# A three-stage kernel (attention, eight experts, gated MLP) with its attention reordered, its index scatters spread, and its MLP weight decoding regrouped

## The chip, the cores and the metric

The kernel runs on one core of one Trainium2 chip. Its time is the device time of one execution in microseconds (us); three runs of the kernel before took 479.15, 480.61 and 486.78 us, median 480.61. The engines are PE (TensorE, matrix products), DVE (VectorE), ACT (ScalarE), POOL (GpSimd) and SP (SyncE, which here only issues transfers). Each takes its instructions in program order.

## The reference

```python
def reference(**kw):
    # 1. linear attention with decay w and bonus u; batch 2, heads 8, 768 tokens, head size 48
    #    y[t] = r[t] @ (state + u*k[t] v[t]^T);  state = w*state + k[t] v[t]^T
    x = attn(r, k, v, w, u)                       # -> 1536 tokens x 384
    # 2. mixture of experts, top 1 of 8, a capacity per expert, hidden 1024
    e, g = argmax(x @ moe_w_gate), softmax value of that expert
    out[i] = g[i] * relu(x[i] @ w1[e[i]]) @ w2[e[i]]      # 0 for tokens over capacity
    # 3. gated MLP, 384 -> 1536 -> 384
    return (sigmoid(out @ w_gate) * (out @ w_val)) @ w_out
```

The three weights of stage 3 come as 64-bit numbers (`wy`, two 32-bit words each), and the kernel decodes them to 32-bit floats on the chip.

## The kernel before

**Attention** works in eight steps `s` (two batches `b` of four head pairs). For each step three tiles are loaded: `dm` (r and k by channel), `kr` (k and r by token) and `v`. `rp` and `kb` scale `dm` by the decay, `pr_part`, `sums` and `diag` build the diagonal term, `kk_part` the keys of the state. On PE `a_mm` makes scores (tile `ap`), `a_cp` copies them on DVE under a mask into `at`, `u_pe`/`u_t` make the running state (`tbd`), `t_mm` and `v_mm` the output, `out_evac`, `out_tr` and `out_x` bring it out and transposed, with router logits `lg` beside it. `r1`, `r2`, `r3` turn the logits of a batch into expert, rank and gate weight; `r4` scales a 128-token block (`xs`) and scatters its rows into the buffer `xs_d` in DRAM, with an indirect DMA issued from POOL. `zinit` first writes zeros there, eight times, in the steps that `ZI` gives. `pre` loads the rows of expert 0 from batch 0 (`xr0`), and `first` adds the ones of batch 1 with 0/1 matrices `pick`, so that expert 0 need not wait for the second batch's scatters. Products with `zero` (`warm_up`, `FILL`) are dummy work for PE.

**Experts**: 64 steps `i` (eight experts of eight slices). Each does `s1` (9 products of 256 columns) and, four steps later, `s2` (9 more). Values are split in a high part (ACT copy) and a low part (subtraction), three products for each. Weight tiles arrive as `raw`; `bg` splits one per step into `rh` (ACT) and `rl` (DVE, in odd steps after 8 POOL); eight are converted ahead. `eload` loads the rows of a later expert (`xr`), `etr` transposes them. `c1`, `c2` compute where each token stands in the sorted order; twelve scatters write the token numbers to `ids_d` (128 numbers of 4 bytes each), one per step from step 4. Beside this the first seven MLP weights (`EARLY`) are decoded, one operation of `decode` per step.

**MLP**: 48 gates, `mf` (18 products of 384 columns), `gate` (`sg` on ACT, `gg` on DVE, `gh` on ACT, `gl` on DVE) and `mo` (9 products). One PSUM pair `pg` serves nearly all gates, so the next `mf` waits for `gg`. Two lanes of gates run skewed by `SKEW` = 2, so the first two rounds hold one gate each. One of the eleven remaining weights is decoded per round: `o1` (ACT), `o2` to `o5` (DVE), `o6` (ACT copy, POOL subtraction), `o7` fetches another weight.

The order is the program's own (`tc.manual_schedule()`).

Of the kernel before, what the change touches and what calls it, by code (L numbers as in the profile page):

```python
# [34 lines left out]
BG = (0, 0, 0, 0, 0, 0, 4, 3)  # L35
DP = 2
ORDER = (0, 1, 2, 12, 3, 4, 13, 5, 6, 14, 7, 8, 15, 9, 10, 16, 11, 17)
EARLY = 7
# [3 lines left out]
R4A = [3, 5]  # L42
R4S = [3]
EB0 = (5, 6)
EB = (1, 4)
# [57 lines left out]
def body(tc, A, out):  # L103
    nc = tc.nc
    E = mybir.EngineType
    with ExitStack() as top, tc.manual_schedule():
# [44 lines left out]
        def decode(n):  # L151
            t = {}

            def o1():
                t["a"] = spl[0].tile([128, 768], F32, tag="wf", name="wf", bufs=2)
                t["i"] = t["a"].bitcast(I32)
                nc.scalar.activation(out=t["a"], in_=r64[n][:, :, 1].bitcast(F32), func=AF.Abs, scale=2.0 ** 16)  # L157
# [27 lines left out]
            return [o1, o2, o3, o4, o5, o6, o7]  # L185
# [20 lines left out]
        tri = gp_.tile([128, 128], BF16, tag="tri", name="tri")  # L206
# [14 lines left out]
        with ExitStack() as ctx:  # L221
# [9 lines left out]
            iw = cat[:, 776:1320].rearrange("p (a x) -> p a x", x=136)  # L231
            wd = cp.tile([112, 4], F32, tag="wd", name="wd")
# [141 lines left out]
            def t_mm(s, fill=0):  # L374
                if s == 7:
                    for g in range(2):
                        y7[g] = ps.tile([128, 512], F32, tag="a", name="y7")
                else:
                    Y0[s] = pb.tile([128, 512], F32, tag="big", name="y0")
# [4 lines left out]
                for c in range(1, 6):  # L384
                    nc.tensor.matmul(y_out(s, c), tbd[s % 2][:, c - 1, :], D[s][:, 0, c * 128:(c + 1) * 128],
                                     start=c in (1, 4) or (s == 7 and c == 2), stop=False, skip_group_check=True)

            def v_mm(s, cs=range(6)):
                for c in cs:
                    o = y_out(s, c)  # L390
                    for h in range(2):
                        nc.tensor.matmul(o[64 * h:64 * h + 64], V[s][:, c, h, :], AT[s][:, slot(c, h), :], start=False,
                                         stop=(h == 1), skip_group_check=True)

# [58 lines left out]
            def r2(b):  # L453
                x, m2, oh, se = R[b]
                rk = ps.tile([128, 6, 8], F32, tag="a", name="rk")
# [10 lines left out]
            def r3(b):  # L466
# [9 lines left out]
                pi = rt.tile([128, 6], I32, tag="pi", name="pi")  # L476
                nc.gpsimd.tensor_scalar_add(pi, pf, 12288.0)
                R[b] = [x, m2, oh, rank, pi, gk]
                pfs[b] = pf

# [4 lines left out]
            def first():  # L485
                x, m2, oh, rank, pi, gk = R[1]
                xk = [pb.tile([128, 512], F32, tag="big", name="xk")[:, 0:256] for _ in range(3)]
# [7 lines left out]
                for c in range(6):  # L495
                    (nc.gpsimd if c > DP else nc.vector).tensor_scalar(
                        out=pick[:, c * 256:c * 256 + 256], in0=cat[:, 512:768], scalar1=pfs[1][:, c:c + 1],
                        scalar2=None, op0=ALU.is_equal)
                hl = []
                for c in range(6):  # L500
# [7 lines left out]
                    if c in R4A:  # L508
                        r4(1, R4A.index(c), "s")
                    nc.vector.scalar_tensor_tensor(out=lo, in0=x[:, c, :], scalar=gk[:, c:c + 1], in1=hi.bitcast(F32),  # L510
                                                   op0=ALU.mult, op1=ALU.subtract)
                order = [(c, kt, p) for b in (0, 2) for p in range(2) for c in (b, b + 1) for kt in range(3)]
# [54 lines left out]
            nc.sync.dma_start(out=cat[:, 512:1320], in_=A["cax"])  # L567
            nc.scalar.dma_start(out=capi, in_=A["cap"][:, 0:1].partition_broadcast(128))
            P_.memset(zero, 0.0)
            for i in range(2):  # L570
                P_.memset(kkd[i][:, :, :, 48:64], 0.0)
# [14 lines left out]
            pr_part(0, (P_, V_))  # L586
# [4 lines left out]
            kb(1, P_)  # L591
            rp(1)
            warm_up(W1)
            u_pe(0)
            u_t(0)
            warm_up(W2)
            pr_part(1, (P_, V_))
            sums(1)
            a_cp(0, ap)
            kk_part(1)  # L600
            diag(1)
            load(2, "v")
            load(3, "k")
            rest = []

            for s in range(8):
# [10 lines left out]
                if s == 0:  # L617
                    kb(2, P_)
                    rp(2)
                    t_mm(0, FILL[0])  # L620
                    ap = a_mm(1)
                    v_mm(0)
                    u_pe(1)
                    pr_part(2, (P_, V_))
                    sums(2)
                    kk_part(2)
                    a_cp(1, ap)
                    diag(2)
                    u_t(1)
                    pr_part(3, (P_, P_))  # L630
                    continue
                out_evac(s - 1)
# [3 lines left out]
                if s > 5:  # L636
                    bg(BG[s], False, 0, rest)
                if s == 7:
                    for o, a, b in rest:
                        nc.vector.tensor_sub(o, a, b)  # L640
# [3 lines left out]
                if nx:  # L644
                    ap = a_mm(s + 1)
                if fu:
                    kb(s + 2, P_)
                    kk_part(s + 2)
                    if s < 5:
                        pr_part(s + 3, (P_, P_))  # L650
                    diag(s + 2)
                if nx:
                    a_cp(s + 1, ap)
                t_mm(s, FILL[s])
# [10 lines left out]
                if s == 5:  # L665
                    r2(0)
                    r3(0)
                    for c in RS[5]:
                        r4(0, c, "v")
                if s == 6:  # L670
                    for o, a, b in rest:
                        nc.vector.tensor_sub(o, a, b)
# [337 lines left out]
```

## Time and profile before

| stretch | us | PE busy | granted clock |
|---|---|---|---|
| attention, to the first product of the experts | 98.07 | 79.59 | 0.91 |
| experts | 143.55 | 138.74 | 0.99 |
| MLP, to the last gate's products | 221.43 | 217.70 | 1.00 |
| last outputs | 15.85 | 10.43 | 0.95 |

The profiled execution took 480.61 us; its span is 478.9 us. PE is busy 446.5 us (93%), DVE 280.6 (59%), ACT 220.8 (46%), POOL 184.5 (39%). A granted clock of 1.00 is TensorE's 2.4 GHz, 0.50 its 1.2 GHz. A line of the timeline gives the start, the duration, the engine, the line of the kernel, and in brackets how long the engine sat idle before it and what ended that.

### The profile page before, as it was taken

The page shows a single profiled execution, that of the slowest core. Times are in us where ns is not written, and L with a number is a line of the kernel's source. Part 1 is how long each engine was busy: PE and PEld are TensorE (multiplying, and loading weights), DVE is VectorE, ACT ScalarE, POOL GpSimd, SP SyncE. Part 2 cuts the span into 40 slices and gives each one's busy share as a digit, 9 for nine tenths or more (in the row PEclk, how much of TensorE's full clock was granted, in tenths as well). Part 3 has the DMA queues.
Part 4 walks back from the last instruction along what each step waited for, and adds up shares of the span by engine and source line. Part 5 has one row for each costly group of instructions (what it writes and reads, how often), then busy time and mean ns, then how long its engine had stood idle before and what let it go on. Part 6 is the DMA issues. An engine that isn't in the chain of part 4 may idle for free.

```text
span 478.9 us, 8621 instructions
## 1 busy us (share of the span) xinstructions
PE 446.5 (93%) x3354; PEld 431.4 (90%) x3356; DVE 280.6 (59%) x474; ACT 220.8 (46%) x450; POOL 184.5 (39%) x127
## 2 busy tenths in 40 slices
PE   6978988599979999999989899999999999999995
PEld 2777987599979999999979799999999999999995
DVE  4797997668778788889347676566222221212221
ACT  2676877536736777675332433433232322222231
POOL 4876938735885647467111311221120200000022
PEclk9979999799989999999999999999999999999999
DMA  7999951779898787773012312310010100000011
GB/s 213 347 340 309 273 203 72 248 288 216 197 227 305 269 271 238 254 258 101 3 47 86 133 66 75 124 68 0 1 49 1 49 1 0 1 1 0 1 50 49
DMA packets 23707, 65.10 MB, mean 136 GB/s; under 512 B 4592, under 2 KB 8816, under 8 KB 23664
## 3 DMA queue, kind: packets, MB, share of 16 engines
q1 hardware_dynamic: 21600, 59.80, 40.5%
q0 software_dynamic: 1920, 4.73, 2.7%
q8 instruction: 27, 0.44, 0.4%
q14 instruction: 16, 0.13, 0.1%
q10 hardware_dynamic: 144, 0.00, 0.0%
HBM read 56.65 MB, written 7.87 MB: 135 GB/s over the span
## 4 chain that ended last, share of the span: by engine, by line
PE 44%; DVE 3%; issue 3%; ACT 1%; POOL 1%; POOLq 0%; DVEq 0%; ACTq 0%
PE pg L936 28%; PE po L960 5%; PE po L959 5%; PE po L958 5%; DVE wf L160 1%; PE ph L825 1%; PE py L848 1%; DVE gg L943 1%; POOL out_dram L190 1%; PE py L849 1%; PE py L850 1%; DVE wf L167 1%; ACT wf L157 1%; DVE wf L171 0%; DVE gl L947 0%
## 5 line engine op out<-in xcount | busy, mean ns | idle before, releaser
L943 DVE TENSOR_TENSOR gg<-sg,pg 128x384 f32<-128x384 f32 x48 | 26.5, 553 | 93.6 <-PE pg L936 91.6
L139 POOL TENSOR_TENSOR rl<-raw,rh 128x768 fp32r<-128x768 f32 x26 | 52.1, 2006 | 36.0 <-ACT rh L137 35.9
L936 PE MATMUL pg<-xhi,ws 128*128 128x384 f32 x240 | 61.6, 337 | 4.6 <-ACT sg L941 3.0
L946 ACT CAST gh<-gg 128x384 fp32r<-128x384 f32 x48 | 24.7, 514 | 83.9 <-DVE gg L943 83.9
L190 POOL DMA_INDIRECT out_dram<-ob,ids x12 | 11.7, 976 | 123.8 <-ACT ob L967 121.4
L941 ACT ACTIVATE sg<-pg 128x384 f32<-128x384 f32 x48 | 23.5, 490 | 70.6 <-PE pg L936 70.6
L848 PE MATMUL py<-hh,rh 128*128 128x256 f32 x192 | 54.6, 284 | 0.0
L137 ACT CAST rh<-raw 128x768 fp32r<-128x768 f32 x64 | 51.4, 836 | 4.7 <-PE py L849 1.9
L849 PE MATMUL py<-hl,rh 128*128 128x256 f32 x192 | 53.5, 279 | 0.0
L850 PE MATMUL py<-hh,rl 128*128 128x256 f32 x192 | 53.5, 278 | 0.0
L139 DVE TENSOR_TENSOR rl<-raw,rh 128x768 fp32r<-128x768 f32 x31 | 46.3, 1497 | 10.6 <-ACT rh L137 10.5
L936 PE MATMUL pg<-xlo,rh 128*128 128x384 f32 x144 | 48.7, 338 | 0.0
L936 PE MATMUL pg<-xhi,rh 128*128 128x384 f32 x144 | 48.6, 338 | 0.0
L936 PEld LDWEIGHTS pg<-xhi,ws 128*128 128x128 f32 x240 | 43.0, 188 | 6.1 <-ACT sg L941 3.7
L936 PE MATMUL pg<-xhi,rl 128*128 128x384 f32 x144 | 48.5, 337 | 0.0
L947 DVE TENSOR_TENSOR gl<-gg,gh 128x384 fp32r<-128x384 f32 x48 | 26.8, 558 | 27.8 <-ACT gh L946 27.8
L936 PE MATMUL pg<-xlo,ws 128*128 128x384 f32 x120 | 40.2, 335 | 0.0
L178 POOL TENSOR_TENSOR rl<-wf,rh 128x768 fp32r<-128x768 f32 x8 | 14.7, 1840 | 65.4 <-ACT rh L177 59.9
L848 PEld LDWEIGHTS py<-hh,rh 128*128 128x128 f32 x192 | 36.4, 189 | 0.1
L850 PEld LDWEIGHTS py<-hh,rl 128*128 128x128 f32 x192 | 36.5, 190 | 0.0
L849 PEld LDWEIGHTS py<-hl,rh 128*128 128x128 f32 x192 | 36.5, 190 | 0.0
L327 ACT ACTIVATE at<-cst,dl 128x128 f32<-128x128 f32 x96 | 28.9, 387 | 7.6 <-DVE dl L319 7.5
(187 smaller groups left out, 1211.9 us busy)
## 6 DMA issues: line engine op xcount, KB each, us to landing
raw<-in_wx_dram SPq DMA_DIRECT2D x64, 384.0 KB, 5.6
r<-in_wy_dram SPq DMA_DIRECT2D x18, 768.0 KB, 4.5
dm<-in_dm_dram SPq DMA_DIRECT2D x8, 672.0 KB, 11.6
kr<-in_kr_dram SPq DMA_DIRECT2D x8, 576.0 KB, 11.6
v<-in_v_dram SPq DMA_DIRECT2D x8, 384.0 KB, 10.9
xs_d<-zero SPq DMA_DIRECT2D x8, 384.0 KB, 10.5
xr<-xs_d SPq DMA_DIRECT2D x8, 384.0 KB, 4.1
cat<-in_cax_dram SPq DMA_DIRECT2D x1, 404.0 KB, 13.8
```

The costliest lines, as they stand in the source:

```text
L137: nc.scalar.copy(out=h, in_=t)
L139: (nc.gpsimd if pool else nc.vector).tensor_sub(rl[n % NR], t, h.bitcast(F32))
L327: nc.scalar.mul(AT[s][:, j, :], ident, dl[:, j:j + 1])
L848: nc.tensor.matmul(y, wh[:, w], hh, start=(f == 0 and m != 1), stop=False, skip_group_check=True)
L849: nc.tensor.matmul(y, wh[:, w], hl, start=False, stop=False, skip_group_check=True)
L850: nc.tensor.matmul(y, wl[:, w], hh, start=False, stop=(f == 7), skip_group_check=True)
L936: nc.tensor.matmul(pg[g], a[:, w], b[kt][:, c], start=(kt == n == 0), stop=(kt == last and n == 2))
L943: nc.vector.tensor_mul(gg, sg, pg[1])
L946: nc.scalar.copy(out=gh, in_=gg)
L947: nc.vector.tensor_sub(gl, gg, gh.bitcast(F32))
L958: nc.tensor.matmul(po[j][t], gh[:, a], wh[:, w], start=(f == 0), stop=False)
L959: nc.tensor.matmul(po[j][t], gh[:, a], wl[:, w], start=False, stop=False)
```

## The change

Settings: the zeros are written in later steps (`ZI`), weights are converted later (`BG`: 2 and 3 instead of 4 and 3), decoding starts at expert step 8 (`T0`), expert 1's rows are transposed at steps 6 and 7 (`EB0`), those of expert 2 two steps later (`EB`). In attention, operations of the first steps move between POOL and DVE and change places, the last step's products change places (`last_open`, `last_t`), batch 0's ranks are made a step earlier in the program's step 5, dummy products (`idle`) come before and after the last ranks, and all `pick` go to DVE. Expert 1's rows are loaded from POOL's queue. The index scatters go to every fourth step from 12. `wf`, the tile of a weight being decoded, gets a third buffer, its low part is made on DVE (`o8`), and the MLP decodes two weights in three gates.

```diff
-T0 = 6
-RS = {5: (0, 1, 2), 6: (3, 4, 5)}
+T0 = 8
+RS = {5: (0, 1), 6: (2, 3, 4, 5)}
+IDLE = (10, 4)
-W2 = 12
-FILL = (0, 4, 4, 4, 4, 4, 4, 8)
-ZI = (4, 4, 0, 0, 0, 0, 0, 0)
+W2 = 20
+FILL = (4, 4, 4, 4, 4, 4, 4, 8)
+ZI = (0, 1, 2, 3, 2, 0, 0, 0)
-BG = (0, 0, 0, 0, 0, 0, 4, 3)
+BG = (0, 0, 0, 0, 0, 0, 2, 3)
-EB0 = (5, 6)
-EB = (1, 4)
+EB0 = (6, 7)
+EB = {1: (3, 6)}
...
-                t["a"] = spl[0].tile([128, 768], F32, tag="wf", name="wf", bufs=2)
+                t["a"] = spl[0].tile([128, 768], F32, tag="wf", name="wf", bufs=3)
...
-                nc.gpsimd.tensor_sub(wyl[n], t["a"], wyh[n].bitcast(F32))
+            def o8():
+                nc.vector.tensor_sub(wyl[n], t["a"], wyh[n].bitcast(F32))
...
             if s == 0:
                     kb(2, P_)
+                    pr_part(2, (P_, P_))
+                    ap = a_mm(1)
+                    t_mm(0, FILL[0])
+                    a_cp(1, ap)
                     rp(2)
-                    t_mm(0, FILL[0])
-                    ap = a_mm(1)
+                    kk_part(2)
                     v_mm(0)
                     u_pe(1)
-                    pr_part(2, (P_, V_))
                     sums(2)
-                    kk_part(2)
-                    a_cp(1, ap)
-                    diag(2)
+                    out_evac(0)
                     u_t(1)
+                    diag(2, 3)
...
                 if nx:
                     ap = a_mm(s + 1)
+                if s == 5:
+                    r2(0, ap[3][:, 256:304].rearrange("p (a b) -> p a b", a=6))
+                    r3(0)
...
             pre()
+            last_open()
+            v_mm(7)
+            for o, a, b in rest:
+                nc.vector.tensor_sub(o, a, b)
+            for g in range(3):
+                last_t(g)
+                last_evac(g)
+            out_tr(6)
+            out_tr(7)
+            xk = [pb.tile([128, 512], F32, tag="big", name="xk") for _ in range(3)]
+            idle(IDLE[0])
+            out_x(6)
             out_x(7)
             r1(1)
...
+                cnt(1)
+                bg(BG[7])
...
-            dops = [op for n in ORDER[:EARLY] for op in decode(n)]
+                dops += [d[0], d[1], d[2], d[3], d[4], d[6], lambda d=d: (d[5](), d[7]())]
-            eload(1)
-            dfetch(ORDER[0])
-            dfetch(ORDER[1])
+            eload(1, nc.gpsimd)
...
-                    if i >= 4 and nid < 12:
+                    if i >= 12 and i % 4 == 0 and nid < 12:
                         scatter(sci, "sci", ids_d, cpos[:, nid:nid + 1], tid[:, nid:nid + 1], 1536)
...
+            def groups():
+                work = [decode(n) for n in ORDER[EARLY:]]
+                a, b = None, None
+                for i in range(0, len(work) + 2, 2):
+                    n, m = (work[j] if j < len(work) else [lambda: None] * 8 for j in (i, i + 1))
+                    yield [n[0]] + ([b[5], a[7]] if a else []) + [n[1], n[2]] + ([b[7]] if a else [])
+                    yield [m[0], n[3], n[4], n[6], m[1]]
+                    yield [n[5], m[2], m[3], m[4], m[6]]
+                    a, b = n, m
...
             for k in range(24 + SKEW):
-                ops = decode(todo.pop(0)) if todo else []
-                for op in ops[:3]:
-                    op()
                 if k < 24:
                     gate(*lane(0, k), mf(*lane(0, k)))
                 if 0 < k <= 24:
                     mo(*lane(0, k - 1))
-                for op in ops[3:5]:
-                    op()
+                if k < 24:
+                    some()
                 b = k - SKEW
                 if b >= 0:
                     gate(*lane(1, b), mf(*lane(1, b)))
+                    some()
```

ACT at the entry of the MLP, before (`xhi` is the last expert's output, `wf` the operation `o1`, `rh` the copy `o6`):

```order
L854 COPY xhi_1303<-py 128x256
L157 ACTIVATE wf<-r_2762 128x768
L941 ACTIVATE sg<-pg 128x384
L946 CAST gh<-gg 128x384
L177 CAST rh_68<-wf 128x768
L157 ACTIVATE wf<-r_2966 128x768
```

The same place on ACT in the change:

```order
L889 COPY xhi_1319<-py 128x256
L979 ACTIVATE sg<-pg 128x384
L984 CAST gh<-gg 128x384
L157 ACTIVATE wf<-r_2799 128x768
L979 ACTIVATE sg<-pg 128x384
L984 CAST gh<-gg 128x384
L157 ACTIVATE wf<-r_3003 128x768
L979 ACTIVATE sg<-pg 128x384
L984 CAST gh<-gg 128x384
L177 CAST rh_68<-wf 128x768
```

The copy of the first weight moved from behind the first gate to behind the third, and no `wf` stands ahead of the first.

DVE at the end of attention, before (`rl` are low parts of expert weights, `lg` the last logits):

```order
L672 TENSOR_TENSOR rl_76<-raw,rh_68 128x768
L672 TENSOR_TENSOR rl_77<-raw,rh_69 128x768
L672 TENSOR_TENSOR rl_78<-raw,rh_70 128x768
L672 TENSOR_TENSOR rl_79<-raw,rh_71 128x768
L640 TENSOR_TENSOR rl_80<-raw,rh_72 128x768
L640 TENSOR_TENSOR rl_81<-raw,rh_73 128x768
L640 TENSOR_TENSOR rl_82<-raw,rh_74 128x768
L425 TENSOR_TENSOR lg<-lg,xp 128x24 x2
```

In the change, the same place and then the start of the experts:

```order
L698 TENSOR_TENSOR rl_76<-raw,rh_68 128x768
L698 TENSOR_TENSOR rl_77<-raw,rh_69 128x768
L412 COPY yt<-y_1092 128x256
L438 TENSOR_TENSOR lg<-lg,xp 128x24 x4
...
L538 TENSOR_TENSOR xel<-xk,xeh 128x256 x3
L552 TENSOR_REDUCE cnts<-oh 128x8
L139 TENSOR_TENSOR rl_78<-raw,rh_70 128x768
L139 TENSOR_TENSOR rl_79<-raw,rh_71 128x768
L139 TENSOR_TENSOR rl_80<-raw,rh_72 128x768
L869 SCALAR_TENSOR_TENSOR hl<-ph,hh 128x512
```

Two subtractions stand ahead of the last logits where seven stood; three moved behind expert 0's rows (`xel`), ahead of the first `hl`.

POOL from the second batch's scatters on, before:

```order
L496 TENSOR_SCALAR pick<-cat,pf 128x256 x3
L190 DMA xs_d<-xs,pi 12288x384 x6
L190 DMA ids_d<-tid,cpos 1536x1 x3
L883 TENSOR_LOAD mxi
L190 DMA ids_d<-tid,cpos 1536x1 x3
L139 TENSOR_TENSOR rl_81<-raw,rh_73 128x768
```

POOL in the change:

```order
L192 DMA xs_d<-xs,pi 12288x384 x6
L830 DMA xr<-xs_d 128x2x384
L921 TENSOR_LOAD mxi
L139 TENSOR_TENSOR rl_81<-raw,rh_73 128x768
L139 TENSOR_TENSOR rl_83<-raw,rh_75 128x768
L192 DMA ids_d<-tid,cpos 1536x1
```

The picks are gone from POOL, the load of expert 1's rows stands in its queue, and the index scatters come one at a time between subtractions.

## Rows read from the trace of the kernel before

**Rows 1.** Stretches: busy time of each engine, clock, DMA share, GB/s.

```profile
0.00:98.07 98.07, 79.59 (x863) 67.33 (x865) 74.14 (x183) 63.88 (x177) 69.83 (x59) 0.91 0.80 254
98.07:241.62 143.55, 138.74 (x1198) 137.57 (x1196) 111.50 (x151) 87.78 (x145) 82.68 (x46) 0.99 0.72 213
241.62:463.05 221.43, 217.70 (x1238) 216.42 (x1239) 92.41 (x136) 65.89 (x123) 27.69 (x19) 1.00 0.11 39
```

**Rows 2.** PE's waits in attention: total us, times, longest.

```profile
PE xk L490 <- DMA xr<-xs_d: 4.4, 1, 4.4
...
PE ap L336 <- DMA v<-in_v_dram: 2.1, 1, 2.1
```

**Rows 3.** PE in order of time, attention: start, duration, line, idle before.

```profile
27.49 3.39 PE L359 MATMUL ap<-dm 48*128 48x128 f32 x24 [2.72 <-DVE at L366]
...
37.26 1.61 PE L359 MATMUL ap<-dm 48*128 48x128 f32 x24
...
46.07 1.61 PE L359 MATMUL ap<-dm 48*128 48x128 f32 x24
...
59.56 1.61 PE L359 MATMUL ap<-dm 48*128 48x128 f32 x24
...
68.12 1.61 PE L359 MATMUL ap<-dm 48*128 48x128 f32 x24
...
74.22 0.61 PE L392 MATMUL t<-at,v 128*64 128x128 f32 x8
...
77.70 1.56 PE L411 MATMUL xp<-cat,yt 128*128 128x136 f32 x12
79.18 1.09 PE L392 MATMUL y<-at,v 128*64 128x128 f32 x16
...
98.07 1.01 PE L825 MATMUL ph<-xeh,rh 128*128 128x256 f32 x3
```

**Rows 4.** Clock in two stretches of 2 us; columns as in Rows 1.

```profile
92.00:94.00 2.00, 2.00 (x11) 2.00 (x11) 0.20 (x1) 0.00 (x0) 1.39 (x3) 0.50 0.95 343
136.00:138.00 2.00, 2.00 (x12) 2.00 (x11) 1.27 (x2) 0.52 (x2) 1.93 (x2) 0.52 1.16 48
```

**Rows 5.** POOL in order of time: a scatter of token rows.

```profile
75.01 6.87 POOL L190 DMA_INDIRECT xs_d<-xs,pi  x1 [0.30 <-issue]
```

**Rows 6.** DVE in order of time, beside that scatter.

```profile
74.87 3.56 DVE L672 TENSOR_TENSOR rl<-raw,rh 128x768 fp32r<-128x768 f32 x4
78.35 2.69 DVE L640 TENSOR_TENSOR rl<-raw,rh 128x768 fp32r<-128x768 f32 x3
```

**Rows 7.** DVE's groups from 82 to 100: busy us, mean ns.

```profile
L510 DVE SCALAR_TENSOR_TENSOR los<-xs,gkp,his 128x384 fp32r<-128x384 f32 x4 | 2.5, 686 | 0.0
...
L496 DVE TENSOR_SCALAR pick<-cat,pf 128x256 fp32r<-128x256 f32 x3 | 0.9, 345 | 0.0
```

**Rows 8.** SP's queue, in order of time: loads of token rows.

```profile
103.10 0.38 SPq L795 DMA_DIRECT2D xr<-xs_d  x1
...
126.13 0.38 SPq L795 DMA_DIRECT2D xr<-xs_d  x1
```

**Rows 9.** PE in order of time, at expert 3's rows.

```profile
135.66 0.52 PE L804 MATMUL xp<-cst,xr 128*128 128x128 f32 x3 [3.20 <-DMA xr<-xs_d]
```

**Rows 10.** Transfers while the index scatters land, and after; columns as Rows 1.

```profile
109.00:146.00 37.00, 33.48 (x280) 33.14 (x279) 27.56 (x36) 22.83 (x38) 26.91 (x18) 0.95 0.96 199
146.00:214.00 68.00, 68.00 (x601) 68.00 (x601) 58.68 (x70) 47.10 (x77) 39.77 (x21) 1.00 0.80 277
```

**Rows 11.** The tile xr, all eight loads of token rows.

```profile
DMA to landing us min/median/max: 3.3/4.1/9.4
```

**Rows 12.** PE's first group of the MLP: busy us, mean ns, idle before.

```profile
L936 PE MATMUL pg<-xhi,ws 128*128 128x384 f32 x240 | 61.6, 337 | 4.6 <-ACT sg L941 3.0 <-DVE xlo L855 0.9 <-DVE gg L943 0.7
```

**Rows 13.** DVE's groups from 241 to 330: busy us, mean ns.

```profile
L160 DVE TENSOR_SCALAR wf<-wf 128x768 f32<-128x768 f32 x11 | 15.8, 1440 | 11.7 <-ACT wf L157 11.7
...
L943 DVE TENSOR_TENSOR gg<-sg,pg 128x384 f32<-128x384 f32 x18 | 9.9, 551 | 7.9 <-PE pg L936 6.0 <-ACT sg L941 1.9
L171 DVE SCALAR_TENSOR_TENSOR wf<-r,wf 128x768 int32<-128x768 int32 x10 | 9.6, 958 | 0.3
```

More of the change, by code (lines that the diff above doesn't have):

```diff
@@ L231, in body @@
             iw = cat[:, 776:1320].rearrange("p (a x) -> p a x", x=136)
+            tri = cp.tile([128, 128], BF16, tag="tri", name="tri")
+            zero2 = cp.tile([128, 128], F32, tag="zero2", name="zero2")
             wd = cp.tile([112, 4], F32, tag="wd", name="wd")
@@ L374, in t_mm @@
             def t_mm(s, fill=0):
[L375 to L379, printed above, removed]
+                Y0[s] = pb.tile([128, 512], F32, tag="big", name="y0")
                 T1[s] = pb.tile([128, 512], F32, tag="big", name="t1")
@@ L393, in v_mm, with last_open, last_t @@
                                          stop=(h == 1), skip_group_check=True)
+            def last_open():
+                for g in range(2):
+                    y7[g] = ps.tile([128, 512], F32, tag="a", name="y7")
+                T1[7] = pb.tile([128, 512], F32, tag="big", name="t1")
+                z = zero2.bitcast(BF16)
+                for o in (y7[0], y7[1], T1[7]):
+                    nc.tensor.matmul(o[:, 0:256], z[:, 0:128], z[:, 0:256], start=True, stop=False, skip_group_check=True)
+            def last_t(g):
+                for c in (2 * g, 2 * g + 1):
+                    if c:
+                        nc.tensor.matmul(y_out(7, c), tbd[1][:, c - 1, :], D[7][:, 0, c * 128:(c + 1) * 128],
+                                         start=False, stop=True, skip_group_check=True)
             def last_evac(g):
@@ L483, in pre, with first @@
                 after(nc.sync.dma_start(out=xr0[0], in_=xs_d[0:256, :].rearrange("(b p) d -> p b d", p=128)), scx)
-            def first():
+            def first(xk3):
                 x, m2, oh, rank, pi, gk = R[1]
-                xk = [pb.tile([128, 512], F32, tag="big", name="xk")[:, 0:256] for _ in range(3)]
+                xk = xk3
                 for b in range(2):
@@ L494, in first, with pickc @@
                 los = wp.tile([128, 12, 128], F32R, tag="at", name="los", bufs=3).rearrange("p a b -> p (a b)")
[L495 to L498, printed above, removed]
+                def pickc(c):
+                    nc.vector.tensor_scalar(out=pick[:, c * 256:c * 256 + 256], in0=cat[:, 512:768],
+                                            scalar1=pfs[1][:, c:c + 1], scalar2=None, op0=ALU.is_equal)
+                pickc(0)
                 hl = []
@@ L590, in body @@
             diag(0)
-            kb(1, P_)
             rp(1)
+            kb(1, V_)
             warm_up(W1)
             u_pe(0)
+            warm_up(W2)
+            load(3, "k")
+            load(2, "v")
+            nc.sync.dma_start(out=cat[:, 512:1320], in_=A["cax"])
+            pr_part(1, (V_, V_))
+            sums(1)
+            diag(1)
+            a_cp(0, ap)
             u_t(0)
[L596 to L599, printed above, removed]
             kk_part(1)
-            diag(1)
-            load(2, "v")
-            load(3, "k")
             rest = []
```

89 lines of the change are left out of this document (46 added, 43 removed).

## The prediction

> **What bounds the kernel now.** I read the stretches first [rows 1]. From the first expert product on, PE is busy 138.74 of 143.55 us and 217.70 of 221.43, nearly all at 2.4 GHz: there only PE's waits can be won. In attention PE is busy 79.59 of 98.07 us at a mean clock of 0.91, so this is the loosest stage. So the second view is PE's waits and its order of time [rows 2, 3]: 4.4 us for expert 0's rows (`xr0`), 2.7 us for the score copies of step 1, 2.1 us for a `v` tile. The third is the clock [rows 4]: after such waits PE works at 1.2 GHz for a while, around 92 and around 136 us. Last come the waits inside the later stages: 3.20 us for expert 3's rows [rows 9], and 4.6 us before `mf` at the start of the MLP, 3.0 of it behind `sg` on ACT [rows 12]. The outputs after the MLP are not touched. The sum is made against the profiled execution, 480.61 us, which is also the median of the three runs.
>
> **The change, part by part.**
>
> *Middle of attention.* The score products of steps 2, 3, 4, 6 and 7 start at 27.49, 37.26, 46.07, 59.56 and 68.12 [rows 3]. Two undisturbed steps, 46.07 to 59.56, take 6.7 us each. Step 37.26 to 46.07 takes 8.81: 2.1 more, the `v` wait [rows 2]. Eight zero writes stood ahead of that load, of 384 KB each; in the change one does, so 2.1 us go. Step 27.49 to 37.26 takes 9.77, 3.0 over: these products run at half speed (3.39 us for 24 where 1.61 is usual). I do not count that won. In the new order `u_t` of step 1 still comes behind a scaling `rp` on DVE, and the nine ACT operations of the next `diag` now wait for `u_t`; my walk through the queues puts the third score products at 36.3 to 37.7, about where they are: 0.3 us. Against it, step 59.56 to 68.12 gets longer: ranks of batch 0 now stand on PE ahead of that step's state products, and on DVE four small operations and two block scalings stand ahead of them: 0.6 us. Sum -1.8; ends -4.5 (the slow clock goes too) and +1 (nothing goes, the ranks cost).
>
> *End of attention.* From the last output product of step 6 (74.22 + 0.61 = 74.8) to the first expert product (98.07) are 23.2 us. Now seven subtractions on DVE, 3.56 + 2.69 us [rows 6], run there, and beside them one scatter of token rows holds POOL 6.87 us [rows 5] until they are done. Expert 0's rows wait for that scatter, PE for the rows, and then works at 1.2 GHz [rows 4]. In the change only two subtractions are left, so the scatters should be through some 6 us earlier and the 4.4 us wait goes. What then sets the pace: on PE 0.3 us of opening products, 1.5 of `v_mm` and 0.8 of `last_t` (both as before), two output transposes of 1.56 [rows 3], so the last logits are there near 80.7; the chain of small operations `r1` to `r3` takes some 2.5 us as it does now, to 83.2. Then DVE makes six picks (345 ns) and six low parts (686 ns) [rows 7], 6.2 us, to 89.4; nine products follow, 1.0 us: 90.4 instead of 98.07. That is -7.7. I take -7.2, since the walk leaves out gaps. Moving three picks from POOL to DVE costs 3 x 0.345 = 1.0, counted in the 6.2. Ends: -9 and -1 (the scatters stay slow; only the shorter order is won).
>
> The row shows the scatter held as long as the subtractions run, 75.01 to 81.88 against 74.87 to 81.04 [rows 5, 6]. The Trainium skill, "SBUF — State Buffer", Who interferes with whom, says that a `tensor_tensor` with both inputs in SBUF blocks only GpSimd work that reads SBUF, and infers that descriptor generation is not blocked. By that rule the scatter was slow for another reason, the wait of 4.4 us would stay and the sum would be 470.2 instead of 465.8; no other row here tells the two apart, and I go by the times.
>
> *Start of the experts.* Three weight conversions move behind expert 0's rows, each 0.89 us on DVE [rows 6], in front of the first `hl`; and expert 1's rows are loaded by POOL, behind six scatters. Before, the load was issued at 103.10, 5.0 us into the stage [rows 8], and used one step earlier than now. In the change the scatters run on past the start of the stage, since low parts and scalings precede them and three subtractions run beside them. By the walk the load lands 11 to 13 us in and is wanted 11 us in: I take +2 (a wait for one subtraction, and 1 us for the rows). Ends 0 and +7.7 (scatters held 6 us as in [rows 5], and a slow clock after it).
>
> *Expert 3's rows.* The load was issued at 126.13 [rows 8] and landed 9.4 us later [rows 11], PE waited 3.20 us and then ran 3.4 us at 0.5 [rows 4, 9], which costs half of that, 1.7: 4.9 in all. While the twelve index scatters land, the transfers move 199 GB/s at a DMA share of 0.96; afterwards 277 at 0.80 [rows 10]. The scatters do slow the others. Spread over steps 12 to 56 they are one in four steps, so I expect this wait gone, -4.9, with +0.8 for a new short one. Ends -5 and 0.
>
> *Decoding in the expert stage.* Seven low parts, 0.95 us each, come to DVE; POOL loses seven. DVE is busy 111.5 of 143.55 [rows 1] and each POOL subtraction now stretches a DVE operation beside it, as `o2` in the MLP, 1440 ns [rows 13] for what takes 0.56 alone: the two cancel, zero. The cover is DVE's 32 idle us; without it up to 6.7.
>
> *MLP.* ACT's copy of a decoded weight waits for DVE, and `sg` stands behind it. Both lanes together hide this; the first two rounds, with one gate each, don't. In the new order the copy comes a gate later. Of the 4.6 us [rows 12] the 0.9 for the last expert's output stays: -3.7. A gate then gives DVE 551 and 558 ns with 0.6 of waiting between, 1.7; two weights in three gates are 2 x (0.56 + 0.56 + 0.95 + 0.96 + 0.95) / 3 = 2.7; 4.4 in a gate's 221.43 / 48 = 4.6. This takes `o2` at 0.56 and not 1440 ns [rows 13]: the longer figure lies beside POOL's subtractions, which are gone. Ends -4.4 and -0.5.
>
> Sum: -1.8 - 7.2 + 2 - 4.9 + 0.8 - 3.7 = -14.8: **465.8 us**.
>
> **Rivals.**
>
> A. *Attention gives little.* If the scatter was slow for another reason than the subtractions, the wait for expert 0's rows stays; and if DVE (74.14 us busy of 98.07 [rows 1], more while POOL works) sets the pace of the steps, the `v` wait only changes its name. Both together leave some -3 of the first two terms' -9.0: 471.8. For it: PE's wait at 27.49 ends on DVE [rows 3]. Against: the other long waits there are for transfers [rows 2].
>
> B. *Expert 1's rows come late from POOL's queue.* Third term +7.7 instead of +2: 471.5. For it: [rows 5]. Against: only three subtractions lie there, not seven.
>
> C. *Slower: each index scatter hits a row load.* Scatters go out at steps 12, 20, 28, 36 and 44, the row loads of experts 3 to 7 at 13, 21, 29, 37 and 45. A load has four steps, 8.2 us (143.55 less some 6 of waits over 67 steps, 2.05 each), until it is used. If a scatter stretches it beyond that, as at 126.13 (9.4 us), PE waits five times 4.9 = 24.5 instead of once: 465.8 - 0.8 + 24.5 = 489.5. It decides at a landing of 8.2 us; the median is 4.1 [rows 11]. Against: at 126 a 768 KB weight and two scatters were under way together. The Trainium skill, "DMA: Bandwidth & Descriptors", Specifications, has writes under 512 B done as read-modify-write; by that each scatter costs the same wherever it lies, and spreading wins nothing in bytes. The trace shows a loss beside scatters [rows 10] but not its kind.
>
> D. *DVE becomes the bound of the decoding MLP.* If a gate with 3.0 us of decoding beside its own 1.7 runs over 4.6 by 0.2 to 0.5, in seven of them, or a transfer is late on ACT, the 3.7 is eaten: 469.5.
>
> **How the numbers follow.** Forecast 0.60; A 0.15, B 0.12, C 0.05, D 0.08. The bound of 2% lies at 471.0 and 490.2, about what a measurement can tell. The forecast's own range is 460 to 470.5, all faster but for a tenth; D mostly faster; A and B lie on the bound and are split, somewhat under half faster; C is half slower, and some chance of an unseen wait joins it. Together: faster 0.72, same 0.24, slower 0.04. The range takes in A, B and D and leaves out C, the best ends of all terms and mishaps together: 459.5 to 475.
>
> **What would show it.** The first expert product near 89 to 91 us instead of 98.07, with no wait for `xr0` and no long scatter in batch 0; no wait for `v`. Expert 3's rows without a wait, and POOL's expert 1 load landing within a microsecond of its use. The first MLP product to the last gate's in some 217 to 218 us instead of 221.43, with `sg` never behind a copy. The prediction is wrong if score products of step 3 stay at 37 and the low parts end after 92, if PE waits at each expert's rows, or if `gg` starts late in every third gate.

## The result, and the profile after

In 20 runs each, the changed kernel takes 485.34 us (median, 484.46 to 488.01) and the kernel before 483.29; the ratio is 1.0069, 95% interval 1.0047 to 1.0091. It is slower by 0.7%, where 465.8 us were forecast. The profiled execution has a span of 483.2 us against 478.9.

The stretches of the changed kernel, as in [rows 1]:

```profile
0.00:89.73 89.73, 78.66 (x884) 64.84 (x886) 71.90 (x183) 60.07 (x170) 52.98 (x50) 0.98 0.80 256
89.73:251.30 161.57, 144.51 (x1198) 142.96 (x1196) 122.36 (x163) 91.78 (x149) 76.10 (x45) 0.95 0.64 201
251.30:467.50 216.20, 216.20 (x1239) 216.20 (x1240) 92.06 (x147) 66.83 (x124) 7.59 (x8) 1.00 0.11 40
```

Attention is 8.3 us shorter, and PE has no idle time left in the MLP. The experts in between take 18.0 us more with the same products. PE's waits up to the MLP (total us, times, longest; `issue` is a wait for nothing that the profile shows), the start of the program aside, against [rows 2] and [rows 9]:

```profile
PE xp L839 <- DMA xr<-xs_d: 13.5, 1, 13.5
...
PE ap L468 <- DVE oh L455: 1.9, 1, 1.9
...
PE ph L860 <- issue: 1.5, 1, 1.5
```

The waits for `xr0`, `v` and expert 3's rows are gone. One wait for expert 1's rows is longer than all three together. POOL in order of time tells where these rows were, against [rows 5]:

```profile
87.98 2.44 POOL L192 DMA_INDIRECT xs_d<-xs,pi  x1 [4.17 <-ACT xs L547]
90.72 0.98 POOL L192 DMA_INDIRECT xs_d<-xs,pi  x1 [0.30 <-issue]
92.00 1.74 POOL L192 DMA_INDIRECT xs_d<-xs,pi  x1 [0.30 <-ACT rh L137]
94.05 0.98 POOL L192 DMA_INDIRECT xs_d<-xs,pi  x1 [0.30 <-DVE rl L139]
95.33 0.98 POOL L192 DMA_INDIRECT xs_d<-xs,pi  x1 [0.31 <-issue]
96.61 2.04 POOL L192 DMA_INDIRECT xs_d<-xs,pi  x1 [0.30 <-issue]
106.63 0.78 POOL L830 DMA_DIRECT2D xr<-xs_d  x1 [7.98 <-issue]
```

And SP's queue, against [rows 8]:

```profile
97.41 0.38 SPq L149 DMA_DIRECT2D r<-in_wy_dram  x1
...
105.94 0.38 SPq L830 DMA_DIRECT2D xr<-xs_d  x1
...
106.88 0.42 SPq L149 DMA_DIRECT2D r<-in_wy_dram  x1
```

The last scatter of token rows ends on POOL at 98.65 us. Both loads that wait for the scatters (expert 1's on POOL, expert 2's on SP) issue only at 106 to 107, so the rows were 7.3 us on their way. The packets show what held them (packets, MB, share of 16 engines; POOL's transfers are in q0, SP's in q1). From 100 to 102 us only SP's move:

```profile
q1 hardware_dynamic: 125, 0.65, 96.2%
```

From 102 to 105.5 the rows of one scatter, 128 of 1.5 KB, go out beside SP's transfers:

```profile
q1 hardware_dynamic: 303, 0.87, 62.9%
q0 software_dynamic: 64, 0.20, 14.5%
```

The load on POOL then needs 7.9 us more, to 114.55 in PE's order of time:

```profile
114.55 0.90 PE L839 MATMUL xp<-cst,xr 128*128 128x128 f32 x3 [13.47 <-DMA xr<-xs_d]
...
236.51 0.28 PE L860 MATMUL ph<-xh,rh 128*128 128x256 f32 x1 [1.51 <-issue]
```

Behind the first of these the granted clock is 0.50 until 117.35, behind the second until 240.2: 2.8 and 3.4 us of work at half speed, 1.4 and 1.7 us lost. What is left of the 18 us shows where PE waits for nothing, in 46 us in the middle of the experts. First the kernel before, then the changed one (columns as in [rows 1]):

```profile
160.00:206.00 46.00, 46.00 (x408) 46.00 (x407) 38.03 (x48) 32.59 (x53) 27.89 (x15) 1.00 0.78 263
```

```profile
160.00:206.00 46.00, 46.00 (x395) 46.00 (x395) 41.71 (x51) 31.73 (x52) 27.06 (x16) 1.00 0.87 255
```

PE is busy throughout at full clock in both, but makes 408 products in one and 395 in the other. The pitch of the products (the time from one to the next) has grown by 3%, from 0.113 to 0.117 us on this average, which over the stage is some 4.5 us by estimate.

Balance: attention -8.3; expert 1's rows 13.5 + 1.4 = 14.9; expert 3's rows -4.9; pitch +4.5; the wait of 1.5 and its clock +3.2; MLP -5.4 (first product to last output product 226.2 us, before 231.5; to the last gate 3.7 of it are idle time and 1.5 shorter PE busy time, which nothing here explains). Sum +4.0; the spans differ by 4.3.

### The profile page after: what moved, and what is told of

Its sections match the earlier page's. It is cut to its first block, busy times and chain, and to the rows that moved or that the text cites. A ratio compares the mean times of both kernels' runs of the same rounds, so it can differ in the third digit from the quotient of the medians.

```text
span 483.2 us, 8654 instructions
## 1 busy us (share of the span) xinstructions
PE 449.7 (93%) x3376; PEld 434.0 (90%) x3377; DVE 288.9 (60%) x497; ACT 221.9 (46%) x448; POOL 140.8 (29%) x106
## 4 chain that ended last, share of the span: by engine, by line
PE 25%; issue 24%; POOL 2%; POOLq 0%; DVE 0%; ACT 0%; DVEq 0%
PE pg L974 15%; PE po L997 2%; PE po L996 2%; PE po L998 2%; POOL out_dram L192 2%; PE ph L860 1%; PE py L883 1%; PE py L885 1%; PE py L884 1%; POOLq L1055 0%; DVE gl L985 0%; DVE gg L981 0%; ACT gh L984 0%; DVE xlo L890 0%; ACT xhi L889 0%
## 5 line engine op out<-in xcount | busy, mean ns | idle before, releaser
L139 POOL TENSOR_TENSOR rl<-raw,rh 128x768 fp32r<-128x768 f32 x26 | 50.2, 1932 | 60.3 <-ACT rh L137 42.4
L139 DVE TENSOR_TENSOR rl<-raw,rh 128x768 fp32r<-128x768 f32 x36 | 44.1, 1237 | 4.2 <-ACT rh L137 4.0
L974 PE MATMUL pg<-xlo,rh 128*128 128x384 f32 x120 | 40.2, 335 | 0.0
L974 PE MATMUL pg<-xhi,rh 128*128 128x384 f32 x120 | 40.2, 335 | 0.0
L974 PE MATMUL pg<-xhi,rl 128*128 128x384 f32 x120 | 40.1, 335 | 0.0
L868 ACT ACTIVATE hh<-ph 128x512 fp32r<-128x512 f32 (+1 forms) x33 | 19.4, 587 | 36.1 <-PE ph L860 35.2
```

Source lines behind the costliest of these rows:

```text
L139: (nc.gpsimd if pool else nc.vector).tensor_sub(rl[n % NR], t, h.bitcast(F32))
L974: nc.tensor.matmul(pg[g], a[:, w], b[kt][:, c], start=(kt == n == 0), stop=(kt == last and n == 2))
```

## Experiments

Ratios are to the kernel before on the same chip, with 95% intervals. Where no other base is named, an edit is one to the changed kernel.

### What made expert 1's rows late

**sp_load**

```diff
-            eload(1, nc.gpsimd)
+            eload(1)
```

> The changed kernel with one difference: expert 1's rows are loaded from SP's queue instead of POOL's, at the same place in the program. Theory: before the change this load stood on SP and held that queue until the scatters of token rows had landed, which kept the weight loads (raw, r) out of the scatters' way; on POOL it holds nothing, and the scatters and the load itself share the DMA engines with about 2 MB of weights. So here the load issues near 103.5 us instead of 106.6 and lands in about 4 us, near 107.5; PE's wait falls from 13.5 to 6 or 7 us, and the time from 485.3 to 477 to 478.5 us. Rival: only POOL's own queue is slow (7.9 us from issue to landing against about 4 on SP); the scatters still land at 105.9, the rows near 110, PE waits about 9.5 us, 481 us. Second rival: neither matters, 485 us.

474.76 us, ratio 0.977 (0.972 to 0.982): by the medians 10.6 us better than the change by one word, and a larger gain than the theory's. SP's queue and PE:

```profile
102.15 0.38 SPq L830 DMA_DIRECT2D xr<-xs_d  x1
```

```profile
105.45 0.90 PE L839 MATMUL xp<-cst,xr 128*128 128x128 f32 x3 [5.44 <-DMA xr<-xs_d]
```

The load issues 4.5 us earlier than on POOL (1.1 of it because the last scatter left POOL earlier, at 97.59) and takes 3.3 us instead of 7.9. A wait of 5.4 us stays. From 99 to 102.1 us the scatters have four packets left, and SP's queue moves nothing:

```profile
q0 software_dynamic: 4, 0.01, 1.8%
```

**late_r**

```diff
-T0 = 8
+T0 = 15
...
-                    if i in (3, 6):
-                        dfetch(ORDER[i // 6])
+                    if i in (10, 13):
+                        dfetch(ORDER[i // 13])
```

> The changed kernel with the two loads r of the first MLP weights (768 KB each) moved from steps 3 and 6 of the experts to steps 10 and 13, and the decoding that needs them from step 8 to step 15; expert 1's load stays on POOL. Theory (weights in the scatters' way): without the first r the scatters land some 2 us earlier and the load is not beside the second r, so PE's wait for expert 1's rows falls from 13.5 to 8 to 10 us: 480 to 482 us. Rival (POOL's queue alone is slow): the wait stays within 1 us of 13.5 and the time at 484.5 to 486 us.

481.58 us, ratio 0.992 (0.989 to 0.995), as the theory said; PE waits 10.1 us. Without the `r` loads the load on POOL issues at 103.87 instead of 106.63, 6.1 us after the last scatter left POOL instead of 8.0, and needs 6.5 us instead of 7.9. The weights do slow the scatters and, it seems, the load.

**pool_held**

```diff
             eload(1, nc.gpsimd)
+            eload(2)
...
-                    if f == 5 and e < 6:
+                    if f == 5 and 0 < e < 6:
```

> The changed kernel, expert 1's load still on POOL, but expert 2's load (SP) moved from step 5 up to the place right behind it, so that SP's queue waits for the scatters again. This parts the two halves of the loss: SP left free, and POOL's own queue. Theory (SP free lets weights in the way): the scatters have landed near 102.5 us instead of 105.9, the load on POOL issues near 103 and, with only expert 2's rows and few weights beside it, lands in 4 to 5 us; PE waits 6 to 8 us instead of 13.5, and the time is 476 to 479 us. Rival (POOL's queue takes 7.9 us whatever else runs): rows at 111, a wait of 9.5 to 10 us, 480 to 482 us.

477.47 us, ratio 0.985 (0.979 to 0.990). POOL and PE:

```profile
102.26 0.78 POOL L830 DMA_DIRECT2D xr<-xs_d  x1 [4.24 <-DVE rl L139]
```

```profile
109.37 0.90 PE L839 MATMUL xp<-cst,xr 128*128 128x128 f32 x3 [9.08 <-DMA xr<-xs_d]
```

The time is the theory's, the wait of 9.1 us nearly the rival's. With SP held again the load issues at 102.3, as in sp_load. From the last scatter's end on POOL to the issue are 4.2 us here, 4.6 in sp_load and 8.0 in the changed kernel, so the freed queue cost 3.4 to 3.8 us. But from POOL the load still takes 7.1 us, against 3.3 from SP. Its first packet leaves 2.4 us after the issue (3.9 in the changed kernel), in sp_load 1.0 us after it. That POOL's queue does this is not shown: expert 2's rows run beside every load from POOL and came 2.6 us behind the one from SP; 384 KB at the 250 GB/s of the stage are, as an estimate, 1.6 us.

**before_pool** (to the kernel before)

```diff
-            eload(1)
+            eload(1, nc.gpsimd)
```

> The kernel before with one difference: expert 1's rows are loaded from POOL's queue instead of SP's. Theory (the load on SP held back the weights): the two r loads (1.5 MB) behind it now go out beside the last scatters and the load, so the scatters land near 106 us instead of 103, the load takes 7 to 8 us, and PE waits 5 to 8 us for rows it needs at 106.9, with a slow clock behind it: 489 to 493 us against 484. Rival (only POOL's queue is slow): the scatters land at 103 as before, the load 7.9 us later at 111, PE waits 4 us: 487 to 488.5 us. Second rival: no difference, 484 us.

487.81 us, ratio 1.014 (1.005 to 1.023), in the rival's band. PE waits 6.7 us, to 110.63; issue is at 105.58, the load takes 5.1 us. Beside before_shift (below), whose experts start at the same 94.9 us and whose SP load goes from 102.93 to 106.17, the issue is 2.7 us later and the load 1.8 us longer, again with expert 2's rows beside it. The first of these is not clear of the difference between profiles: the issue comes 4.6 us after the last scatter left POOL, in before_shift 1.9, but in the kernel before 4.7 as well.

### The pitch of the products

**shift** (the same instructions, tiles 128 bytes lower)

```diff
-                mx = rt.tile([128, 6], F32, tag="mx", name="mx")
+                mx = rt.tile([128, 14], F32, tag="mx", name="mx")[:, 0:6]
...
-                eq = rt.tile([128, 6, 8], F32, tag="eq", name="eq")
+                eq = rt.tile([128, 6, 8], F32, tag="eq", name="eq", bufs=1)
```

> The changed kernel with every tile that is allocated behind the small tiles of the router moved down by 128 bytes (eq gets one buffer, mx 32 bytes more), so that xh, xl, hh and hl start again at a multiple of 512 plus 288 bytes, as in the kernel before, and not plus 416; the instructions are the same. Theory: the start address of the moving operand sets the pitch of the experts' products; the pitch goes back from 0.1175 to 0.1135 us, over some 1150 products a gain of 4 to 5 us: 480.5 to 481.5 us. Rival: the pitch depends on something else (other traffic, order of instructions) and stays: 485 us.

485.98 us, ratio 1.003 (1.001 to 1.005). The pitch goes back (median of the blocks of nine products 0.1134 us, 0.1178 in the changed kernel; the expectations have 0.1137 and 0.1175), and the time does not: the rival's time at the theory's pitch. PE now waits 15.2 us for expert 1's rows, 1.0 for a later expert's, 0.8 for DVE's `rl` and 2.6 behind the overflow branch.

**before_shift** (to the kernel before, tiles 128 bytes higher)

```diff
-                mx = rt.tile([128, 6], F32, tag="mx", name="mx")
+                mx = rt.tile([128, 22], F32, tag="mx", name="mx")[:, 0:6]
```

> The kernel before with the tiles behind the router's small ones moved up by 128 bytes (mx takes 64 bytes more in each of its two buffers), so that xh, xl, hh and hl start at a multiple of 512 plus 416, as in the changed kernel; the instructions are the same. Theory: the experts' products go at a pitch of 0.1175 instead of 0.1137 us, 3 to 5 us more, less what the wait for expert 3's rows gives back: 486 to 488.5 us. Rival: the pitch in the changed kernel came from its other traffic and order; here it stays 0.1137: 484 us.

486.07 us, ratio 1.005 (1.002 to 1.009), at the lower end of the theory. The same 46 us as above:

```profile
160.00:206.00 46.00, 46.00 (x396) 46.00 (x396) 38.18 (x48) 32.22 (x53) 26.27 (x14) 1.00 0.77 258
```

396 products, as in the changed kernel, with DVE as little busy as before. So the place of the tiles sets the pitch in both directions. Which operand's address it is, was not tried.

**best1** (sp_load, shift and sp_line together)

> The changed kernel with three edits: expert 1's load on SP, the tiles moved down by 128 bytes, the 28 shorter dummy products. Theory: the pitch goes back to 0.1137 us (4 to 5 us), of which new waits for DVE (19 of 20 us busy in the middle of the experts when the products go faster) take 1 to 3: 468.5 to 470.5 us. Rival: DVE and the transfers bound the experts as soon as the products go faster, and all of the gain is lost, as in the run with the tiles moved alone: 471.5 to 473 us.

478.89 us, ratio 0.990 (0.985 to 0.996): worse than sp_load and than both forecasts. Most blocks of nine go at 0.1134 us, and the experts still take 155.1 us, with waits of 3.8 (expert 1's rows), 1.1, 0.6 (`rl`) and 4.1 us (behind the branch). DVE and POOL before one of the slow places:

```profile
215.71 4.36 DVE L167 SCALAR_TENSOR_TENSOR wf<-r,wf 128x768 int32<-128x768 int32 x1
```

```profile
215.60 3.64 POOL L139 TENSOR_TENSOR rl<-raw,rh 128x768 fp32r<-128x768 f32 x2
```

A DVE operation that mostly takes 0.95 us lasts 4.4 beside two POOL subtractions. That the long pitch had covered this is likely, not shown.

### The parts by themselves

**before_mlp** (the kernel before with the change's `groups`, three `wf`, `o8`; room made by `ti = tb.bitcast(I32)` and one buffer for `eq` and `tm`)

```diff
-tag="wf", name="wf", bufs=2)
+tag="wf", name="wf", bufs=3)
...
-                nc.gpsimd.tensor_sub(wyl[n], t["a"], wyh[n].bitcast(F32))
+            def o8():
+                nc.vector.tensor_sub(wyl[n], t["a"], wyh[n].bitcast(F32))
```

> The kernel before with the MLP part of the change alone: a third buffer for wf, the low part of a decoded weight on DVE (in the experts too), and two weights decoded in three gates; 1024 bytes of small tiles are given up for the buffer, so that all tiles behind it keep their places modulo 512. Theory: the MLP gets as short as in the changed kernel, 221.4 to about 216 us, and nothing else moves: 483.3 to about 478 us. Rival: the lower part in the experts loads DVE and gives back 1 to 3 us there: 479 to 481 us.

476.67 us, ratio 0.981 (0.976 to 0.987), somewhat better than the theory. First to last product of the MLP 226.7 us instead of 231.5, though the wait for expert 3's rows grew to 6.4 us in its profile.

**mlp_spread** (before_mlp with spread index scatters)

```diff
-                    if i >= 4 and nid < 12:
+                    if i >= 12 and i % 4 == 0 and nid < 12:
```

> The kernel before_mlp (the kernel before with the MLP part of the change alone, 476.7 us) with the index scatters at every fourth step from 12, as in the change. Theory: the wait for expert 3's rows (6.4 us in before_mlp) and half of the 6.8 us at half clock behind it go: 467.5 to 471 us. Rival: the wait only moves to a later expert's rows: 474.5 to 477 us.

473.11 us, ratio 0.977 (0.973 to 0.981). No wait for any `xr` in the experts, which take 140.0 us instead of 147.0. The time fell by less than expected; attention is 1 us longer in its profile.

**sp_dense** (sp_line with the line of mlp_spread undone)

> The kernel sp_line (expert 1's load on SP, 28 shorter dummy products) with the twelve index scatters put back one per step from step 4. Theory: while they land, expert 3's rows (issued at step 13) take 9 us instead of 4 and PE waits 2 to 6 us at step 17, with the half clock behind it: 476 to 480 us against 472.6. Rival: the wait before the change came from the r loads (768 KB each), which lie elsewhere now; no wait at expert 3 and 472 to 474 us.

478.86 us, ratio 0.989 (0.985 to 0.993), 1.2% (some 6 us) more than sp_line. PE:

```profile
120.04 0.52 PE L839 MATMUL xp<-cst,xr 128*128 128x128 f32 x3 [2.62 <-DMA xr<-xs_d]
...
154.70 0.52 PE L839 MATMUL xp<-cst,xr 128*128 128x128 f32 x3 [2.17 <-DMA xr<-xs_d]
```

The first wait is for expert 2's rows (expert 3's were expected): their load, issued at 104.32 among the scatters, landed 15.6 us later. The second, for expert 4's, comes when the last index scatter, of 132.65, is long done, so it is not shown to be theirs. The time is in the theory's band: close index scatters cost some us, and spreading them is worth about what the prediction said.

### The wait behind the branch

**sp_line** (sp_load, and)

```diff
-IDLE = (10, 4)
+IDLE = (20, 8)
...
-xk[0][:, 256:512], z[:, 0:128], z[:, 0:256]
+xk[0][:, 256:384], z[:, 0:128], z[:, 0:128]
```

> The changed kernel with expert 1's load on SP, and with the 14 dummy products of 256 columns around the last ranks made 28 of 128 columns, which puts 14 more products into PE's program ahead of the branch at the overflow code and no more work. Theory: the wait of 1.7 us six products behind that branch is PE's own program being fetched: 16 KB come in 1.5 us just then, and PE needs the next 16 KB six products on. 14 products more put the border just ahead of the branch's end, and the wait and the half clock behind it (1.7 us) go: 471 to 472.5 us against 474.8 with the load on SP alone. Rival: the wait comes from the 1536 transfers of 4 bytes (ids) that are under way then; it stays: 474 to 475.5 us.

472.63 us, ratio 0.977 (0.972 to 0.982); the wait behind the branch is gone, while the ratio is that of sp_load. In its profile attention ended 4.2 us later (a `v` wait of 2.2 us among it), but that execution, of 476.2 us, is the longest of the five, so a gain in time is not shown. The page names queue 8 as instruction transfers: 16 KB came at 233.7 in the changed kernel, 2.2 us behind the branch. But in shift and best1, where the products go faster, the wait is 2.6 and 4.1 us, in best1 with the same PE program as here. In the changed kernel, sp_load, late_r, pool_held, shift, best1 and one_behind such a transfer starts 2.0 to 3.9 us behind the branch and the wait ends 2.2 to 3.4 us after that start; here it starts 0.2 us ahead of the branch. Fetching is the likely cause, not shown, nor is what sets its start.

### Versions

**best2** (best1 with the low parts of the experts' decoding on POOL: `nc.gpsimd.tensor_sub`)

> The kernel best1 (load on SP, tiles moved down by 128 bytes, 28 shorter dummy products; 478.9 us) with the low parts of the first seven MLP weights back on POOL, seven DVE operations of 0.95 us less in the experts. Theory (with the short pitch DVE is the bound of the experts): DVE's 19 of 20 us fall to about 18, the waits for rl and the half clock behind them go, the experts shrink from 155 to 148 to 150 us: 472 to 474.5 us. Rival: each POOL operation holds up the DVE operation beside it by as much as it saves: 477.5 to 480 us.

Ratio 0.998 (0.995 to 1.002): beyond the rival's end; relieving DVE by POOL did not pay. Its times spread from 479.1 to 489.5 us, and nothing here rests on its profile.

**bg43_shift** (sp_load and shift) and **bg43_line** (sp_line), both with

```diff
-BG = (0, 0, 0, 0, 0, 0, 2, 3)
+BG = (0, 0, 0, 0, 0, 0, 4, 3)
```

> The changed kernel with expert 1's load on SP, the tiles moved down by 128 bytes, and BG 4 and 3 again (two more conversions before the last attention outputs, two fewer left for the experts). Theory (DVE lacked a reserve): attention 1.5 to 2 us longer than in sp_load, no waits for rl in the experts, pitch 0.1137; the experts fall from 153 to 143 to 146 us: 466 to 470 us. Rival (DVE is bound by the decoding, not by the start): waits for rl as in best1, experts 151 to 155 us, 475 to 479 us.

> The kernel sp_line (load on SP, 28 shorter dummy products, tiles where the change has them) with BG 4 and 3 again. With the long pitch of 0.1175 us DVE has its reserve anyway, so two more conversions ahead bring nothing in the experts and cost 1.5 us in attention, less a shorter hold of the last scatters: 472 to 474.5 us, if the first theory of the run beside it holds. Rival (the conversions beside the scatters were the loss): expert 1's wait falls from 3.9 to 1 us: 468 to 470 us.

472.77 us, ratio 0.979 (0.974 to 0.984), and 474.35, 0.982 (0.975 to 0.989). The experts take 149.7 and 150.4 us. With the long pitch conversions ahead bring nothing, as the theory said. With the short one the time lies between theory and rival: 5.4 us less in the experts than in best1, from which it also differs in the dummy products, and not the 143 to 146 us of the theory. They were at most part of what was missing. Expert 1's rows are there at 105.4 and 106.8.

**one_behind** (sp_load, shift, and `BG` 4 and 1)

> The changed kernel with expert 1's load on SP, the tiles moved down by 128 bytes, and BG 4 and 1: two of the three conversions beside batch 1's scatters are made before the last outputs of attention. Theory: the scatters of batch 1 are held 1.5 to 2 us less, the rows of expert 1 land near 104 instead of 105.4 and PE waits 1 to 2 us instead of 3.1: 470 to 472 us against 472.8. Rival: the landing is set by the transfers that share the DMA engines, not by the hold: rows at 105.5, 472 to 474.5 us.

474.61 us, ratio 0.979 (0.973 to 0.985), at the upper end of the rival's band. Yet its profile has no wait for expert 1's rows: the last scatter ends at 96.6, expert 1's load issues at 99.06, and the experts take 146.9 us. In this profile the hold beside the conversions did set the landing; waits of 1.7 us for `xr0` in attention and 2.4 behind the branch came instead.

**three_behind** (mlp_spread, and)

```diff
-EB0 = (5, 6)
+EB0 = (6, 7)
...
-                if s > 5:
-                    bg(BG[s], False, 0, rest)
-                if s == 7:
-                    for o, a, b in rest:
-                        nc.vector.tensor_sub(o, a, b)
+                if s == 6:
+                    bg(BG[6], False, 0, rest)
...
             cnt(1)
+            bg(BG[7])
```

> The kernel mlp_spread (kernel before with the new decoding and the spread index scatters, 473.1 us) with the second group of three conversions moved from ahead of the last attention outputs to behind expert 0's rows, and expert 1's rows transposed at steps 6 and 7 instead of 5 and 6. Theory: batch 0's scatter is held to 78.4 instead of 82 us, expert 0's rows are there when wanted and the 4.8 us wait and half of the 6.8 us at half clock go; expert 1's rows land near 105.5, as everywhere, and are wanted at 106 now: attention 98 to 94, experts unchanged at 140 to 142, 467.5 to 470 us. Rival: whatever attention wins is lost waiting for expert 1's rows: 472 to 474 us.

470.90 us, ratio 0.969 (0.962 to 0.976): the best of all, 3% under the kernel before, without the new attention. POOL and DVE, against [rows 5] and [rows 6]:

```profile
75.28 4.26 POOL L192 DMA_INDIRECT xs_d<-xs,pi  x1 [0.30 <-issue]
```

```profile
75.13 3.56 DVE L671 TENSOR_TENSOR rl<-raw,rh 128x768 fp32r<-128x768 f32 x4
```

Four subtractions instead of seven beside the scatter, and it is held to 79.5 instead of 81.9 us. Attention ends at 94.2, as expected, though a wait of 2.6 us for `xr0` stays (4.8 in mlp_spread), and no `xr` is waited for in the experts (142.0 us).

## Why the prediction was wrong

**The step that failed** is "Start of the experts": +2 us, with ends 0 and 7.7, where it came to 14.9. The load was to land 11 to 13 us into the stage, on a walk that followed POOL's instructions and added one held subtraction and 1 us for the rows. It landed 24.8 us in. Three things were wrong in it:

- Issue was taken for landing. The last scatter left POOL 8.9 us into the stage, near the walk; its rows took 7.3 us more. The rows that show such a delay were there: before, the load issued at 103.10 [rows 8] behind scatters of which the last had left POOL by 98.4:

```profile
97.46 0.97 POOL L190 DMA_INDIRECT xs_d<-xs,pi  x1 [0.30 <-issue]
```

- A load that waits at the head of SP's queue also holds the weights behind it. Moved to POOL, it let `raw` and `r` out beside the scatters. pool_held gives 3.8 us for this (the issue comes 4.2 us after the last scatter left POOL, instead of 8.0). The prediction asked who waits behind the load on POOL, not who no longer waits behind it on SP.
- A load from POOL was priced like one from SP. It took 7.9 us here and 7.1 in pool_held, 3.3 from SP in sp_load: 3.8 to 4.6 us. How much of this is POOL's queue and how much expert 2's rows beside it stays open.

Rival B had the place and the sign right; its price of 7.7 was half of what came, since it priced only the hold.

**Middle and end of attention** were right in sum: -1.8 and -7.2 were forecast, and the last score products start 2.5 us earlier (65.61), the first expert product 8.3 (89.73, in the forecast's 89 to 91), so the end brought 5.8. In the middle this was partly luck. From the score products of step 2 to those of step 3 it took 8.20 us instead of 9.77, at a clock of 1.00 instead of 0.68; this slow clock was not counted as won. The step of the `v` wait got 1.1 us shorter, not 2.1. And the gain was not kept. Expert 1's rows come at 104.4 to 107.9 us in the SP versions with the new attention, one_behind aside; in sp_load the MLP starts at 241.5 us, before at 241.6. Nor is it the same in every run: in before_shift and before_pool the held scatter is another one (3.4 us instead of 6.87), PE does not wait for `xr0`, and attention ends at 94.9.

On the held scatter, the time of the rows decided rightly against what the Trainium skill infers in "SBUF — State Buffer", Who interferes with whom: three_behind takes away three of the seven subtractions and the hold shrinks with them. In before_shift a scatter is held from 77.80 to 81.20 us, behind four subtractions that end at 80.35. Rival A did not happen.

**Expert 3's rows**, -4.9 and +0.8: right, the wait is gone and no new one came; sp_dense brings one of 2.6 us back beside the scatters. Rival C did not happen. The Trainium skill's rule in "DMA: Bandwidth & Descriptors", Specifications, on small writes would leave their cost as it is wherever they lie; no run here shows how they are written, and sp_dense shows that their place decides whether a row load waits.

**Decoding in the experts**, zero: with the decoding alone changed, in before_mlp, DVE is busy 119.1 us in the experts instead of 111.5, so the two do not cancel. In the changed kernel it is 122.4, with conversions that came over from attention. PE shows nothing of it there, but waits 0.8 and 0.6 us for `rl` in shift and best1, where the products go faster. What hid it was likely the long pitch, which the prediction did not know.

**MLP**, -3.7: right; all idle time before PE's products went but the 0.9 us, which is the 3.7. The other 1.7 of the 5.4 us were in no term. Rival D did not happen.

**Not in the sum:** the pitch (4.5 us), from the place that the tiles have in the change, and the wait behind the branch (3.2 with its clock). The first is shown from both sides, though in shift its end alone did not shorten the time; the second's cause stays open.

## What to carry to other kernels

When a transfer moves to another queue, look at both queues: what stood behind it was held back too, and its release can cost more than the wait that was removed. Price a chain of scatter and load from issue to landing, not by the engine's instructions. A gain ahead of a chain with its own earliest end is only a longer wait at that end, so first ask when the next thing needed will be there.

## What the runs showed of the hardware

- A 384 KB load of token rows took 3.3 us from SP's queue (sp_load) and 5.1 to 7.9 us from POOL's (before_pool, late_r, pool_held, the changed kernel), there always with a second such load beside it. Its first packet left 1.0 us after the issue from SP and 2.4 to 3.9 us after it from POOL.
- The same products go at 0.1134 or 0.1178 us as tiles lie 128 bytes lower or higher, with nothing else changed (shift, before_shift). Within a kernel single stretches switch between the two values.
- POOL subtractions of 128x768 stretched a DVE operation beside them: 0.95 us became 4.36 beside two, which together last 3.64 (best1).
- A scatter that POOL issues while DVE subtracts back to back was held until 0.85 us after the last subtraction: 6.87 us beside seven (the kernel before), 4.26 (three_behind) and 3.40 (before_shift) beside four.
